# Feed-forward layers with features on partitions, and transposing DMAs in place of TensorE transposes

## The chip, the cores and the metric

The kernel runs on one core of one Trainium2 chip. The metric is the device time of one execution in microseconds (us). Before the change the median of three runs is 1394.78 us (1393.33 to 1395.5).

## The reference: what is computed

The kernel computes a forward pass and all gradients of a stack of four residual layers, alternately linear attention (A) and a gated feed-forward layer (B), with shared weights: layers 0 and 2 are A, 1 and 3 are B. There are 2048 tokens (S), 512 model features (D), 1376 hidden features (F), all tensors in bf16. Cut to what matters here:

```python
def _B_ref(x, w_gate, w_up, w_down):
    g = jnp.einsum("bsd,df->bsf", x, w_gate)
    u = jnp.einsum("bsd,df->bsf", x, w_up)
    h = _sigmoid(g) * u
    return jnp.einsum("bsf,fd->bsd", h, w_down)

x = x + _A_ref(_layernorm(x), A_wqkv, A_wo)
x = x + _B_ref(_layernorm(x), B_w_gate, B_w_up, B_w_down)
x = x + _A_ref(_layernorm(x), A_wqkv, A_wo)
x = x + _B_ref(_layernorm(x), B_w_gate, B_w_up, B_w_down)
```

Outputs are x, the gradient of x, and the gradients of the five weight matrices (summed over the two layers that share each).

## The kernel before, in words

[...] A matmul loads its stationary operand (`lhsT`, up to 128 columns) and streams its moving operand (`rhs`, up to 512 columns) past it.

The phases in the order of the program: `a_fwd(0)`, `b_fwd(1)`, `a_fwd(2)`, `b_fwd(3)`, then backward `b_bwd_p1(3)`, `a_bwd_p1(2)`, `b_bwd_p2(3)`, `b_bwd_p1(1)`, `a_bwd_p2(2)`, `a_bwd_p1(0)`, `b_bwd_p2(1)`, `a_bwd_p2(0)`. The p1 phases carry the gradient of the activations back, the p2 phases form weight gradients from tensors that earlier phases stored in DRAM.

**Feed-forward, forward (`b_fwd`, 16 tiles per layer).** For each token tile the normalised input stands transposed in `hT` (features on partitions, 128 tokens wide). `hT` is the stationary operand, and the weights `wg` and `wu` move in slices of 512, 512 and 352 columns (L621, L624): tokens come out on partitions. ScalarE makes the sigmoid and its complement (L626, L628), VectorE the product hh (L629), GpSimd a factor for the backward pass (L630). The down projection (L599) contracts over F, and so needs F on partitions: 11 TensorE transposes per tile (L587) with copies by ScalarE (L590, L592) turn `hh_t` into `hhT`. The rows go to DRAM as `ssd` and `hdd`, tokens by features.

**Feed-forward, backward (`b_bwd_p1`, 16 tiles per layer).** The same scheme: `gT` is stationary, `wdT` moves (L760), VectorE makes two products `dd` (L762, L763), 22 transposes per tile (L728) with ScalarE copies (L730, L732) make `ddT`, and 22 matmuls of 512 columns (L742) contract over F. `dd` goes to DRAM next to hh, tokens by features.

**Weight gradients (`b_bwd_p2`).** They contract over tokens, and so need tokens on partitions, as they stand in DRAM. Six groups of feature chunks (five of 256 features, one of 96), each with three sets `p_set` (hh, du, dg): 2048 rows of up to 512 bytes, 1 MB in a full set, loaded by plain DMAs on the SP queue (L811) into a pool of three buffers. A full set feeds 32 matmuls of 512 columns (L863) or 64 of 256 (L833).

**Transposed weights.** The backward pass needs all five weight matrices transposed. During the two `a_fwd` phases, `wT_groups` transposes them on TensorE (L372, L396, 196 transposes in 49 groups of four), copies them out of PSUM on VectorE and ScalarE (`evac`) and stores them to DRAM; `load_b_weights` and `load_a_weights` load them by plain DMAs at the start of the p1 phases. One buffer each is shared by `wuT` and `wqkvT`, and by `wgT` and `woT`.

**What sets the order.** The program is written phase by phase, but a planner at build time makes the final order on each engine from dependences, priorities (earlier in the program first) and assumed costs. Work of a p2 phase can therefore stand between the instructions of a p1 phase, and does (L863 among L742). On the chip each engine, and each DMA queue, goes through its list in order: an instruction that waits holds up all that follows it in that list, so a load on SP stands behind the stores before it.

Of the kernel before, what the change touches and what calls it, by code (L numbers as in the profile page):

```python
# [16 lines left out]
S = 2048  # L17
# [33 lines left out]
def kernel(  # L51
# [70 lines left out]
    for l in range(4):  # L122
        d = {}
        d["h"] = dram.tile([S, D], BF16, name=f"sv_h{l}")
        d["gbf"] = dram.tile([S, D], BF16, name=f"sv_gbf{l}")
        if l % 2 == 0:
            for nm in ("pq", "pk", "v", "o"):
                d[nm] = dram.tile([S, D], BF16, name=f"sv_{nm}{l}")
            d["dqkv"] = dram.tile([S, 3 * D], BF16, name=f"sv_dqkv{l}")
        else:  # L130
            d["ssd"] = dram.tile([S, 2, F], BF16, name=f"sv_ssd{l}")
            d["hdd"] = dram.tile([S, 3, F], BF16, name=f"sv_hdd{l}")
        k.sv[l] = d
    k.wT = dict(
        wqkvT=dram.tile([3 * D, D], BF16, name="wqkvT_d"),
        woT=dram.tile([D, D], BF16, name="woT_d"),
        wgT=dram.tile([F, D], BF16, name="wgT_d"),
        wuT=dram.tile([F, D], BF16, name="wuT_d"),
        wdT=dram.tile([D, F], BF16, name="wdT_d"),
    )  # L140
# [11 lines left out]
    with tc.tile_pool(name="wfwd", bufs=1) as wfwd:  # L152
# [17 lines left out]
        with ExitStack() as lctx:  # L170
            k.lnres = dict(
                stg=lctx.enter_context(tc.tile_pool(name="ln_stg", bufs=2)),
                hT=lctx.enter_context(tc.tile_pool(name="ln_hT", bufs=4)),
# [4 lines left out]
            if phases != "fwd":  # L178
                wtg = wT_groups(k)
                half = 26  # L180
                with tc.tile_pool(name="wt_stage", bufs=2) as wt_stage:
                    a_fwd(k, 0, lns[0], nxt=lns[1],
                          extra=lambda ps_pool: [g(wt_stage, ps_pool) for g in wtg[:half]])
                b_fwd(k, 1, lns[1], nxt=lns[2])
                with tc.tile_pool(name="wt_stage2", bufs=2) as wt_stage:
                    a_fwd(k, 2, lns[2], nxt=lns[3],
                          extra=lambda ps_pool: [g(wt_stage, ps_pool) for g in wtg[half:]])
            else:
                a_fwd(k, 0, lns[0], nxt=lns[1])
                b_fwd(k, 1, lns[1], nxt=lns[2])  # L190
                a_fwd(k, 2, lns[2], nxt=lns[3])
# [17 lines left out]
    with ExitStack() as bctx:  # L209
# [3 lines left out]
        def load_b_weights():  # L213
            k.wdT = wb.tile([P, NDC, F], BF16, name="wdT", tag="w_c")
            nc.sync.dma_start(out=k.wdT[:], in_=k.wT["wdT"].rearrange("(c p) f -> p c f", p=P))
            k.wuT = wb.tile([P, NFC, D], BF16, name="wuT", tag="w_a")
            k.wgT = wb.tile([P, NFC, D], BF16, name="wgT", tag="w_b")
            for t_sb, t_d in ((k.wuT, k.wT["wuT"]), (k.wgT, k.wT["wgT"])):
                nc.sync.dma_start(out=t_sb[:, 0:NFC - 1, :],
                                  in_=t_d[0:(NFC - 1) * P, :].rearrange("(c p) j -> p c j", p=P))  # L220
                nc.sync.dma_start(out=t_sb[0:FLAST, NFC - 1, :], in_=t_d[(NFC - 1) * P:F, :])

        def load_a_weights():
            k.woT = wb.tile([P, NDC, D], BF16, name="woT", tag="w_b")
            nc.sync.dma_start(out=k.woT[:], in_=k.wT["woT"].rearrange("(c p) j -> p c j", p=P))
            k.wqkvT = wb.tile([P, 3 * NDC, D], BF16, name="wqkvT", tag="w_a")
            nc.sync.dma_start(out=k.wqkvT[:], in_=k.wT["wqkvT"].rearrange("(c p) j -> p c j", p=P))
# [4 lines left out]
                  sets=bctx.enter_context(tc.tile_pool(name="p2sets", bufs=3)),  # L232
# [113 lines left out]
def wT_groups(k):  # L346
    nc = k.nc
    groups = []
    cnt = [0]

    def evac(dst, src):
        if cnt[0] % 2 == 0:
            nc.vector.tensor_copy(dst, src)
        else:
            nc.scalar.copy(dst, src)
        cnt[0] += 1

    for w_sb, wT_d, C in ((k.wg, k.wT["wgT"], F), (k.wu, k.wT["wuT"], F),
                          (k.wqkv, k.wT["wqkvT"], 3 * D), (k.wo, k.wT["woT"], D)):
        ncc = (C + P - 1) // P  # L360
        for cc0 in range(0, ncc, 4):
            ccs = list(range(cc0, min(cc0 + 4, ncc)))
            holder = {}
            for j, cc in enumerate(ccs):
                def g(stage, ps_pool, w_sb=w_sb, wT_d=wT_d, C=C, cc0=cc0, ccs=ccs, j=j, cc=cc, holder=holder):
                    if j == 0:
                        holder["t"] = stage.tile([P, 4, D], BF16, name="wt_st")
                    st_t = holder["t"]
                    r = min(P, C - cc * P)
                    ps = ps_pool.tile([P, NDC, P], BF16, name="wt_ps")  # L370
                    for rc in range(NDC):
                        nc.tensor.transpose(ps[0:r, rc, :], w_sb[:, rc, cc * P:cc * P + r], k.ident[:])  # L372
                    evac(st_t[0:r, j, :], ps[0:r, :, :].rearrange("p a b -> p (a b)"))
                    if j == len(ccs) - 1:
                        nfull = len([c_ for c_ in ccs if min(P, C - c_ * P) == P])
                        if nfull > 0:
                            nc.sync.dma_start(
                                out=wT_d[cc0 * P:(cc0 + nfull) * P, :].rearrange("(n p) d -> p n d", p=P),
                                in_=st_t[:, 0:nfull, :])
                        if nfull < len(ccs):  # L380
                            c_ = ccs[nfull]
                            r_ = C - c_ * P
                            nc.sync.dma_start(out=wT_d[c_ * P:c_ * P + r_, :], in_=st_t[0:r_, nfull, :])
                groups.append(g)
    for cc in range(NDC):
        holder = {}
        for fs in range(3):
            def g(stage, ps_pool, cc=cc, fs=fs, holder=holder):
                if fs == 0:
                    holder["t"] = stage.tile([P, F], BF16, name="wdt_st")  # L390
                st_t = holder["t"]
                fcs = fchunks_of_slice(fs)
                ps = ps_pool.tile([P, NDC, P], BF16, name="wt_ps")
                for i, fc in enumerate(fcs):
                    r = fc_rows(fc)
                    nc.tensor.transpose(ps[:, i, 0:r], k.wd[0:r, fc, cc * P:(cc + 1) * P], k.ident[0:r, 0:r])  # L396
                c0, w = FSL[fs]
                evac(st_t[:, c0:c0 + w], ps[:].rearrange("p a b -> p (a b)")[:, 0:w])
                if fs == 2:
                    nc.sync.dma_start(out=k.wT["wdT"][cc * P:(cc + 1) * P, :], in_=st_t[:])  # L400
            groups.append(g)
    return groups


NPRE = 2


class FwdLN:
# [7 lines left out]
    def stage(self, st):  # L416
# [10 lines left out]
        hT = R["hT"].tile([P, NDC, P], BF16, name="hT")  # L427
        transpose_blocks(k, R["ps"], hT[:], [h_t[:, c * P:(c + 1) * P] for c in range(NDC)], "vector", tag="ln_tp")
        self.hTs[st] = hT
# [5 lines left out]
    def pop(self, st):  # L435
        self.ensure(st)
        return self.hTs.pop(st)


def a_fwd(k, l, ln, nxt=None, extra=None):  # L440
    nc, tc = k.nc, k.tc
    sv = k.sv[l]
    with ExitStack() as ctx:
# [8 lines left out]
        if extra is not None:  # L452
            ps_extra = ctx.enter_context(tc.tile_pool(name=f"af_ps_extra{l}", bufs=1, space=PSUM))
# [656 lines left out]
```

## Time and profile before

| what | us |
|---|---|
| median of three runs | 1394.78 |
| the profiled execution: span from first to last instruction | 1393.1 |
| TensorE matmul busy | 1297.9 (93%) |
| VectorE busy | 679.9 (49%) |
| ScalarE busy | 647.3 (46%) |
| GpSimd busy | 250.5 (18%) |
| mean granted TensorE clock | 0.988 |
| mean DMA rate | 194 GB/s, 269.77 MB moved |

No time outside the span is on record for the profiled execution; its span stands 1.7 us below the median of the runs.

How to read the views: a row of the timeline has the start and the length in us, the engine (PE is TensorE, PEld its weight loads, DVE VectorE, ACT ScalarE, POOL GpSimd, SPq the queue of SyncE), the line of the kernel, the operation, output and inputs, the shape (partitions by columns) and the number of instructions merged into the row; a bracket tells how long the engine had been idle before and who released it. The length of a PE row includes the pipeline's tail of its last matmul; how long a group holds TensorE is read from its start to the start of the next row. A DMA row has the size of one transfer and the median time from issue to landing.

### The profile page before, as it was taken

Reading aid. Unit: us, or ns where it says so; the run is one execution under the profiler, and the core shown is the slowest. Engines: PE = TensorE matmul, PEld = TensorE weight load, DVE = VectorE, ACT = ScalarE, POOL = GpSimd, SP = SyncE. Lnnn points to the kernel's source line nnn. Section 1 sums busy time; section 2 is a strip of 40 time slices with the busy share of each in tenths; the row PEclk is TensorE's granted clock in tenths of the full one; section 3 lists DMA queues with packets and bytes.
Section 4 is the critical chain, followed back from the end, with each engine's and each line's share of the span. In section 5 each row is a group of like instructions: output and inputs, shape, how many; then the busy total and the mean of one; then the engine's idle time right before and its main releaser. Section 6 shows DMA issues by size and latency. Waiting matters only on the chain. (4 is left out here: it accounts for less than half of the span.)

```text
span 1393.1 us, 25045 instructions
## 1 busy us (share of the span) xinstructions
PE 1297.9 (93%) x9956; PEld 790.1 (57%) x9956; DVE 679.9 (49%) x1468; ACT 647.3 (46%) x1168; POOL 250.5 (18%) x413
## 2 busy tenths in 40 slices
PE   4989899998899898998999999999999999988988
PEld 2555455556455444554665677555548675556767
DVE  6664644567533355665857400456640676611111
ACT  5857576775776544443547411444431447600000
POOL 4026654105633300002100100010010101100000
PEclk9999999999999999999999999999999999999999
DMA  7622334452543497547774586964568956499745
GB/s 273 230 103 103 149 152 158 147 177 98 201 178 143 169 326 259 175 168 237 218 230 148 181 227 149 334 217 167 172 199 248 275 169 192 143 311 261 175 122 162
DMA packets 268853, 269.77 MB, mean 194 GB/s; under 512 B 24576, under 2 KB 245184, under 8 KB 268736
## 3 DMA queue, kind: packets, MB, share of 16 engines
q1 hardware_dynamic: 246272, 253.50, 57.2%
q10 hardware_dynamic: 22464, 14.68, 3.6%
q8 instruction: 78, 1.28, 0.4%
q14 instruction: 39, 0.32, 0.1%
HBM read 144.57 MB, written 123.57 MB: 192 GB/s over the span
## 5 line engine op out<-in xcount | busy, mean ns | idle before, releaser
L730 ACT COPY ddT<-T_ps 128x1024 bf16<-128x1024 bf16 (+1 forms) x96 | 83.1, 867 | 103.4 <-PE T_ps L728 103.3
L630 POOL TENSOR_TENSOR ssd_t<-hh_t,oms 128x512 bf16<-128x512 bf16 (+1 forms) x96 | 100.6, 1052 | 83.0 <-ACT oms L628 48.4
L648 DVE SCALAR_TENSOR_TENSOR junk<-t_sb,h_ld 128x512 bf16<-128x512 f32 x64 | 46.1, 720 | 137.6 <-ACT t_sb L646 136.6
L762 DVE TENSOR_TENSOR dd_t<-dhh_ps,ssd_ld 128x512 bf16<-128x512 f32 (+1 forms) x96 | 60.4, 629 | 102.0 <-PE dhh_ps L760 102.0
L742 PEld LDWEIGHTS <-ddT 128*128 128x128 bf16 (+1 forms) x704 | 66.3, 98 | 71.4 <-issue 12.5
L468 PE MATMUL mm_ps<-wqkv,hT 128*128 128x512 bf16 x384 | 100.2, 386 | 0.5 <-DVE x_108 L601 0.4
L742 PE MATMUL dh_ps<-wuT,ddT 128*128 128x512 bf16 (+1 forms) x352 | 96.5, 382 | 3.9 <-ACT t_sb L646 0.9
L833 PE MATMUL p_ps<-p_set,p_a_15354 128*128 128x256 bf16 (+1 forms) x768 | 82.5, 267 | 10.8 <-DVE dw_stg L798 10.8
L629 DVE TENSOR_TENSOR hh_t<-u_ps,ssd_t 128x512 bf16<-128x512 f32 (+1 forms) x96 | 60.7, 634 | 65.3 <-PE u_ps L624 50.3
L760 PE MATMUL dhh_ps<-wdT,gT 128*128 128x512 bf16 (+1 forms) x384 | 87.8, 364 | 5.0 <-DMA wdT<-wdT_d 4.3
L624 PE MATMUL u_ps<-wu,hT 128*128 128x512 bf16 (+1 forms) x384 | 92.4, 361 | 0.0
L621 PE MATMUL g_ps<-wg,hT 128*128 128x512 bf16 (+1 forms) x384 | 92.0, 361 | 0.4 <-DVE ostage L530 0.4
L833 PE MATMUL p_ps<-p_set,p_a_10151 128*128 128x256 bf16 (+1 forms) x768 | 81.5, 261 | 0.9 <-DMA p_set<-sv_hdd_130 0.9
L599 PE MATMUL y_ps<-wd,hhT 128*128 128x512 bf16 (+1 forms) x352 | 81.4, 380 | 0.0
L742 PE MATMUL dh_ps<-wgT,ddT 128*128 128x512 bf16 (+1 forms) x352 | 81.3, 379 | 0.0
L833 PEld LDWEIGHTS <-p_a_15354 128*128 128x128 bf16 x768 | 68.9, 100 | 21.7 <-issue 8.4
L590 ACT COPY hhT<-hhT_ps 128x512 bf16<-128x512 bf16 (+1 forms) x96 | 49.5, 515 | 58.3 <-PE hhT_ps L587 58.1
L728 PEld LDWEIGHTS <-dd_t 128*128 128x128 bf16 (+1 forms) x704 | 50.7, 101 | 40.8 <-DVE dd_t L762 18.5
L833 PEld LDWEIGHTS <-p_a_10151 128*128 128x128 bf16 x768 | 67.2, 98 | 9.2
L728 PE MATMUL T_ps<-ident,dd_t 128*128 128x128 bf16 (+1 forms) x704 | 66.4, 221 | 3.6 <-DVE dd_t L762 3.5
L838 DVE TENSOR_TENSOR dw_stg<-p_ps,dw_stg 128x512 bf16<-128x512 f32 (+1 forms) x36 | 23.4, 653 | 87.5 <-PE p_ps L833 74.4
L1038 PE MATMUL dh_ps<-wqkvT,dkvT 128*128 128x512 bf16 x256 | 65.6, 380 | 0.0
(493 smaller groups left out, 2498.3 us busy)
## 6 DMA issues: line engine op xcount, KB each, us to landing
p_set<-sv_hdd_130 SPq DMA_DIRECT2D x15, 1024.0 KB, 7.1
p_set<-sv_hdd_119 SPq DMA_DIRECT2D x15, 1024.0 KB, 6.3
sv_ssd_118<-ssd_t SPq DMA_DIRECT2D x16, 688.0 KB, 3.1
sv_ssd_129<-ssd_t SPq DMA_DIRECT2D x16, 688.0 KB, 3.1
ssd_ld<-sv_ssd_129 SPq DMA_DIRECT2D x16, 688.0 KB, 5.5
sv_hdd_130<-dd_t SPq DMA_DIRECT2D x16, 688.0 KB, 3.9
ssd_ld<-sv_ssd_118 SPq DMA_DIRECT2D x16, 688.0 KB, 6.0
sv_hdd_119<-dd_t SPq DMA_DIRECT2D x16, 688.0 KB, 3.7
```

What stands on the lines that cost most here:

```text
L468: nc.tensor.matmul(ps[:], lhsT=hT[:, kc, :], rhs=k.wqkv[:, kc, n * D:(n + 1) * D], start=(kc == 0), stop=(kc == NDC - 1))
L599: nc.tensor.matmul(y_ps[:], lhsT=T["hhT"][0:r, fc, :], rhs=k.wd[0:r, fc, :], start=(fc == 0), stop=(fc == NFC - 1))
L621: nc.tensor.matmul(g_ps[:, 0:w], lhsT=hT[:, kc, :], rhs=k.wg[:, kc, c0:c0 + w], start=(kc == 0), stop=(kc == NDC - 1))
L624: nc.tensor.matmul(u_ps[:, 0:w], lhsT=hT[:, kc, :], rhs=k.wu[:, kc, c0:c0 + w], start=(kc == 0), stop=(kc == NDC - 1))
L629: nc.vector.tensor_tensor(hh_t[:, c0:c0 + w], u_ps[:, 0:w], ssd_t[:, 0, c0:c0 + w], ALU.mult)
L630: nc.gpsimd.tensor_tensor(ssd_t[:, 1, c0:c0 + w], hh_t[:, c0:c0 + w], oms[:, 0:w], ALU.mult)
L728: nc.tensor.transpose(tps[0:r, a, i, :], dd[:, a, fc * P:fc * P + r], k.ident[:])
L730: nc.scalar.copy(ddT[:, :, fcs[0]:fcs[0] + nfull, :], tps[:, :, 0:nfull, :])
L742: nc.tensor.matmul(dh_ps[:], lhsT=T["ddT"][0:r, a, fc, :], rhs=wT[0:r, fc, :], start=(i == 0), stop=(i == n_mm - 1))
L760: nc.tensor.matmul(dhh_ps[:, 0:w], lhsT=gT[:, jc, :], rhs=k.wdT[:, jc, c0:c0 + w], start=(jc == 0), stop=(jc == NDC - 1))
L833: nc.tensor.matmul(psv[:, icl, :], lhsT=lhs_all[:, st, ic * P:(ic + 1) * P], rhs=set_t[:, st, 0:W], start=(st == 0), stop=(st == NST - 1))
L1038: nc.tensor.matmul(dh_ps[:], lhsT=lhsT, rhs=k.wqkvT[:, n * NDC + c, :], start=(i == 0), stop=(i == 3 * NDC - 1))
```

## The change

Four things are changed at once.

1. `b_fwd` works on blocks of 512 tokens (`SB`), `b_bwd_p1` on blocks of 256 (`SBB`). The weight chunks are now stationary and the tokens move, so features come out on partitions, and the transposes of hh, du and dg are gone. hh, sg, qg, du and dg are stored in DRAM as features by tokens.
2. `b_bwd_p2` loads its sets from there with `dma_start_transpose` on the SP queue, in a pool of two buffers instead of three.
3. `wT_groups` is gone; the transposed weights are loaded by `dma_start_transpose` straight from the inputs. Since F is no multiple of 128, two small DRAM tensors `wtail` are filled at the very start by four DMAs.
4. Smaller: `NPRE` 4 instead of 2 (tiles whose layer norm is made ahead), three blocks of `hT` instead of four tiles, other counts of PSUM buffers.

```diff
+    k.wtail = {nm: dram.tile([D, P], BF16, name=f"wtail_{nm}") for nm in ("wg", "wu")}
+    for nm, w_in in (("wg", B_w_gate), ("wu", B_w_up)):
+        nc.sync.dma_start(out=k.wtail[nm][:, 0:FLAST], in_=w_in[:, F - FLAST:F])
+        nc.sync.dma_start(out=k.wtail[nm][:, FLAST:P], in_=w_in[:, 0:P - FLAST])
...
-            nc.sync.dma_start(out=k.wdT[:], in_=k.wT["wdT"].rearrange("(c p) f -> p c f", p=P))
+            nc.sync.dma_start_transpose(out=k.wdT[:], in_=B_w_down[:, :])
...
+            for t_sb, w_in, nm in ((k.wuT, B_w_up, "wu"), (k.wgT, B_w_gate, "wg")):
+                nc.sync.dma_start_transpose(out=t_sb[:, 0:NFC - 1, :], in_=w_in[:, 0:(NFC - 1) * P])
+                nc.sync.dma_start_transpose(out=t_sb[:, NFC - 1, :], in_=k.wtail[nm][:, :])
...
-                  sets=bctx.enter_context(tc.tile_pool(name="p2sets", bufs=3)),
+                  sets=bctx.enter_context(tc.tile_pool(name="p2sets", bufs=2)),
...
# b_fwd
+        for sb in range(NSB):
+            hT = ln.pop_block(sb)
...
+            for fc in range(NFC):
...
-                    nc.tensor.matmul(u_ps[:, 0:w], lhsT=hT[:, kc, :], rhs=k.wu[:, kc, c0:c0 + w],
+                    nc.tensor.matmul(u_ps[0:r, :], lhsT=k.wu[:, kc, fs], rhs=hT[:, kc, :],
                                      start=(kc == 0), stop=(kc == NDC - 1))
...
-                if fs >= 1:
-                    transposes(T, fs - 1)
+                if fc in (2, 4, 6, 8):
+                    j = (fc - 2) // 2
+                    if prev is not None:
+                        finish(prev, j)
+                    if sb + 1 < NSB:
+                        ln.ensure((sb + 1) * NB + j)
+            for nm in ("sg", "qg", "hh"):
+                frows_dma(k, sv[nm], sb * SB, T[nm], True)
...
# b_bwd_p1
+            for fp in range(0, NFC, 2):
+                fcs = [fc for fc in (fp, fp + 1) if fc < NFC]
+                r = fc_rows(fcs[-1])
+                n = len(fcs)
+                dhh_ps = ps_dhh.tile([P, 2, SBB], F32, name="dhh_ps")
+                for i, fc in enumerate(fcs):
+                    for jc in range(NDC):
+                        nc.tensor.matmul(dhh_ps[0:r, i, :], lhsT=k.wdT[:, jc, fc * P:fc * P + r], rhs=gT[:, jc, :],
+                                         start=(jc == 0), stop=(jc == NDC - 1))
+                nc.vector.tensor_tensor(T["du"][0:r, fp:fp + n, :], dhh_ps[0:r, 0:n, :], sg[0:r, fp:fp + n, :],
+                                        ALU.mult)
...
+                if fp in (2, 6):
+                    j = (fp - 2) // 4
+                    if prev is not None:
+                        finish(prev, j)
+                    if (sb + 1) * SBB < S:
+                        g_stage((sb + 1) * NBB + j)
...
-def p2_set(k, R, src2d, c0, w):
+def p2_set(k, R, src2d, c0, w, transposed=False):
     t = R.sets.tile([P, NST, R.set_w], BF16, name="p2_set")
+    if transposed:
+        k.nc.sync.dma_start_transpose(out=t[:, :, 0:w], in_=src2d[c0:c0 + w, :])
+        return t
```

## The prediction, as it was put on record

> **What bounds the kernel.** I read the page's busy times first, then the timeline of TensorE inside one tile of each stage that the change rewrites, then the transfers that take over the transposing.
>
> ```profile
> PE 1297.9 (93%) x9956; PEld 790.1 (57%) x9956; DVE 679.9 (49%) x1468; ACT 647.3 (46%) x1168; POOL 250.5 (18%) x413
> PE   4989899998899898998999999999999999988988
> ```
>
> TensorE is busy for 93% of the span, in nearly every slice; the other engines stay near half. So what counts is how long the removed instructions hold TensorE, from a row's start to the next row's start. One forward tile:
>
> ```profile
> 214.94 0.40 PE L587 MATMUL hhT_ps<-ident,hh_t 128*128 128x128 bf16 x4
> 215.18 0.76 PE L621 MATMUL g_ps<-wg,hT 128*128 128x352 bf16 x4
> ...
> 216.37 0.39 PE L587 MATMUL hhT_ps<-ident,hh_t 128*128 128x128 bf16 x4
> 216.59 2.54 PE L599 MATMUL y_ps<-wd,hhT 128*128 128x512 bf16 x11
> 218.97 0.33 PE L587 MATMUL hhT_ps<-ident,hh_t 128*128 128x128 bf16 x3
> 219.14 0.39 PE L318 MATMUL ln_tp<-ident,hstage 128*128 128x128 bf16 x4
> ```
>
> The reader is to see that there is no idle bracket: each transpose pushes back what follows. The groups hold TensorE for 0.24, 0.22 and 0.17 us, 0.63 per tile. One backward tile (its groups stand at 572.05, 576.31, 576.98, 577.80 and 578.24 us; two of them):
>
> ```profile
> 572.05 0.50 PE L728 MATMUL T_ps<-ident,dd_t 128*128 128x128 bf16 x6
> 572.39 0.39 PE L318 MATMUL gT_ps<-ident,gstage 128*128 128x128 bf16 x4
> ...
> 577.80 0.39 PE L728 MATMUL T_ps<-ident,dd_t 128*128 128x128 bf16 x4
> 578.02 0.38 PE L742 MATMUL dh_ps<-wuT,ddT 128*128 128x512 bf16 x1
> ```
>
> They hold it for 0.34, 0.24, 0.22, 0.22 and 0.22: 1.24 us per tile. Last, a weight-gradient phase, and the loads that feed it between 812 and 868 us:
>
> ```profile
> 826.01 7.07 PE L863 MATMUL p_ps<-p_a_10156,p_set 128*128 128x512 bf16 x32
> 832.92 14.14 PE L833 MATMUL p_ps<-p_set,p_a_10151 128*128 128x256 bf16 x128
> 846.89 7.07 PE L863 MATMUL p_ps<-p_a_10156,p_set 128*128 128x512 bf16 x32
> ```
> ```profile
> p_set<-sv_hdd_130 SPq DMA_DIRECT2D x6, 1024.0 KB, 6.0
> p_set<-sv_hdd_130 SPq DMA_DIRECT2D x3, 384.0 KB, 4.0
> ```
>
> A set of 1 MB is used up in 6.9 to 7.0 us, without a pause between sets, and its load lands 6.0 us after issue (4.0, 5.9 and 7.1 at least, median and most, over all nine). With three buffers a load has two sets' time, 13.9 us, to arrive.
>
> **Transposes taken off TensorE.** 32 forward tiles x 0.63 = 20.2 us; 32 backward tiles x 1.24 = 39.7; the weights' 49 groups of four, at 0.22 each (a row at 40.21, the next at 40.43), 10.8. Sum 70.7 us. TensorE's recorded waits in front of them (L587 6.8, L728 3.6) total 10.4; something else will be late at some of these places, so I count half, 5. The ScalarE copies behind them, the `evac` copies and the stores of the transposed weights go too; they lie beside TensorE's work and count for nothing, nor is any cover lost with them.
>
> **Columns added.** From the rows above 512 columns cost 0.216 us (6.91 us / 32) and 256 cost 0.109 (13.97 / 128), so more weight loads per column cost almost nothing. Forward, a block of four tiles streams 88 x 512 = 45056 columns instead of 8 x 1376 x 4 = 44032, because the last chunk of 96 features costs a whole pass: 1024 more in each of 8 blocks, 3.5 us. Backward 44 x 256 = 11264 instead of 11008 in each of 16 blocks, 1.7 us, and 704 matmuls at 1 ns over the half price, 0.7. Together +6.
>
> **Start.** Four DMAs are put on SP ahead of the first load of x, on which the first LayerNorm waits. SP's rows there take 0.39 to 0.48 us each, so at least 1.8 us if nothing else is behind. They move 2048 short rows; the row nearest to that is the 384 KB set, 2048 rows of 192 bytes, at 4.0 us. If the planner puts them later, nothing. Bounds 0 and 5, I take 3.
>
> **Transposed sets, the unknown.** No row shows a transposing DMA. Its result has 128 tokens on partitions, so I assume that each row of 2048 tokens is read in 16 pieces of 256 bytes: 4096 pieces where the plain load has 2048 of 512. The two rows above differ only in bytes: 2.0 us for 640 KB, and 2.8 us for 2048 pieces and everything fixed. The shortest landing in the issue view is 2.2 us; with that as the fixed part, 2048 pieces are worth 0.6 us and a transposed set lands in 6.6. From below: 6.0, as a plain one; no gain, because the bytes are the same. From above: the rate of the 192-byte set, 4.0 x 1024 / 384 = 10.7 us. I take 6.6, nearest to the row of the same size.
>
> With two buffers a load is issued when its buffer is used up, 0.2 us after the set's end (812.04 to 812.23), and is needed one set later: it may take 6.7. The median then just fits, but plain landings reach 1.2 us over their median; I take 0.6 us of stall per set, 30 full sets in both layers, +18 (bounds 0 and (10.7 - 6.7) x 30 = 120). The six small sets are used up in 2.7 to 3.5 us and land in about 4.6: 1.3 x 6 = 8; half is hidden, where the next phase's matmuls can be put between: +4.
>
> [...]
>
> **Transposed weights.** At the start of the backward pass TensorE waits for `wdT`, whose plain load lands in 6.7 us:
>
> ```profile
> 489.47 3.14 PE L760 MATMUL dhh_ps<-wdT,gT 128*128 128x512 bf16 x7 [4.33 <-DMA wdT<-wdT_d]
> ```
>
> Scaled by 6.6 / 6.0, that is 0.7 us more. `wuT` and `wgT` follow on the same queue; at 1 MB in 6.6 - 2.2 = 4.4 us the three (4 MB) are in about 19.5 us after 482.8, at 502. The first block's 44 matmuls and two pairs of the next take about 7 us from 490, so `wgT` is wanted at about 499: 4 us. In layer 1 the loads were issued at 633, long ahead. Two attention phases start with `woT`: 1 us each. Together +7, bounds 0 and 20 (10.7 in place of 6.6).
>
> **What I cost at nothing.** Stores and loads of features by tokens move the same bytes in shorter rows; the DMA engines are 66% busy in that stage (487 to 640 us), and the cover is TensorE's block of 14.7 us. In a backward block VectorE has six pairs of products (0.60 us per full instruction) and two LayerNorm chains (2.3 us each), 12.1 us with the casts, against 14.7 on TensorE; three buffers of `dhh_ps` are the cover. The layer norms of a forward block, four now before its first matmul, are hidden by the block before, whose matmuls last 28 us.
>
> **Sum.** Against the profiled span: 1393.1 - 70.7 - 5 + 6 + 3 + 18 + 4 + 7 = 1355.4. The median of the runs lies 1.7 above that span: 1357 us.
>
> **Rivals.**
> (1) All transfers are hidden: only the transposes, their waits and the columns count, 1393.1 - 70.7 - 10.4 + 6 = 1318, 1320 on the scale of the runs. For it: TensorE has other phases' work to put between (L863 stands among L742 at 572.61). A tile of the backward stage also lasts 9.23 us (569.67 to 578.90) where its rows hold TensorE for about 8.75, and if that gap goes in 16 tiles more is gained, 8 us: down to about 1310.
> (2) VectorE becomes the bound of the backward stage: it goes in order, and its chain waits on ScalarE and GpSimd (3.05 us in front of L648 at 582.34). If 1 us per block is lost, 16 blocks give 16 us: 1373. Against it: 49% busy.
> (3) The other side, slower: transposed loads take longer than a set's compute. The place is `b_bwd_p2`, where the third buffer is gone. Without the +18 the sum is 1339, so the gain is used up at 55 us, 1.8 us per set, a landing over 8.5 us. At 10.7 it is 1393.1 - 70.7 + 6 + 5 + 20 + 120 + 8, 1481, 1483 on the scale of the runs. For it: plain loads keep the engines 69% busy in this phase already, the pieces are shorter, and SP works in order, so a transpose that occupied SP would also hold back the stores and the partial gradients behind it (TensorE already waits 5.49 us at 1260 for such a chain). Against it: only an unseen cost makes it.
> (4) The change does not take what it says off TensorE, if the planner had put the transposes in idle time: 1393. The rows without brackets speak against it.
>
> **Chances.** The forecast with its surroundings (1340 to 1366) 0.38; (1) 0.20; (2) and smaller stalls up to 1391, 0.09; (4), within 0.2% (about what a measurement of this kernel tells from no change), 0.03; (3) 0.30, of which a third lies beyond its price. The range goes from 1310 to 1483 and leaves out some 15 in 100. Faster 0.67, same 0.03, slower 0.30.
>
> **What would show it.** L587, L728, L372 and L396 are gone, and TensorE's busy time is some 65 us or more lower. L811 shows a landing: below 6.7 us rival (1), 6.7 to 8.5 the forecast, above rival (3), with idle time of L833 and L863 put down to `p_set`. Idle time of L760 put down to VectorE would be rival (2). I am wrong in kind if TensorE's stalls grow inside the forward stage, or if plain transfers land later because transposes are in flight.

## The result: slower by half a per cent, where 2.7% less time was forecast

The changed kernel takes 1400.95 us (median of ten runs, 1397.8 to 1406.23), the kernel before 1394.74 us on the same chip (1391.82 to 1397.98): a ratio of 1.0045, 95% interval 1.0028 to 1.0062. The forecast was 1357, its range 1310 to 1483; the chance given to slower was 0.30.

The profiled execution spans 1396.9 us, 3.8 more than before. First the page's busy times and two rows of its timeline:

```profile
PE 1234.9 (88%) x8960; PEld 750.9 (54%) x8960; DVE 666.1 (48%) x1435; ACT 497.4 (36%) x871; POOL 250.2 (18%) x405
...
PE   3978999997999389998989889999989999749888
...
PEclk9989999999999789999999999999999999979999
```

TensorE's busy time fell by 63.0 us, near the forecast ("some 65 us or more"; 64.7 without the waits), though at a lower mean granted clock, 0.967 where it was 0.988 before. But its idle time inside the span grew from 95 to 162 us. Two holes are new, the 3 in the fourteenth slice (about 454 to 489 us) and the 7 and 4 around 1220 us, and in both the granted clock falls too, to 0.71 in the first and to 0.73 between 1225 and 1260 us. The view of TensorE's waits names what ended the idle time (us in total, times, longest):

```profile
PE gT_ps L303 <- DMA gstage<-in_grad_out_dram: 27.5, 1, 27.5
PE p_ps L781 <- DMA p_set<-sv_dg: 24.5, 8, 11.4
...
PE p_ps L811 <- DMA p_set<-sv_hh: 10.3, 2, 9.3
```

Before, TensorE waited 0.9 us for sets in all, and for no load of a gradient tile:

```profile
PE p_ps L833 <- DMA p_set<-sv_hdd_130: 0.9, 1, 0.9
```

After, with 5.3 us for `du`, the sets make TensorE wait 40 us; the first gradient tile of the backward pass makes it wait 27.5. Where the time is gained and lost is seen from the ends of TensorE's work in each stage. The last column is an experiment told below, in which no DMA transposes anything:

| stage | before, us | after | difference | nothing transposed by DMA |
|---|---|---|---|---|
| start to the end of the last forward block | 482.8 | 465.8 | -17.0 | 460.5 |
| from there to the first `dhh` matmul | 6.7 | 30.1 | +23.4 | 14.9 |
| `b_bwd_p1(3)`, to its last `dh` | 153.1 | 127.2 | -25.9 | 126.5 |
| `a_bwd_p1(2)` | 145.1 | 154.6 | +9.5 | 144.3 |
| `b_bwd_p2(3)` | 89.1 | 104.7 | +15.6 | 89.4 |
| `b_bwd_p1(1)` | 151.4 | 122.2 | -29.2 | 123.5 |
| `a_bwd_p2(2)`, `a_bwd_p1(0)` | 188.6 | 195.0 | +6.4 | 192.3 |
| `b_bwd_p2(1)` and the last phase | 172.4 | 192.7 | +20.3 | 174.2 |

(Weight-gradient work that stood between a p1 phase's matmuls moved to the next stage: 5.0 us of the first -25.9, L863, and 6.5 of the -29.2, L885.) The rewritten backward stages gained at least what they should, by the count of the prediction 18.7 us each. The time is lost at the start of the backward pass, in `a_bwd_p1(2)`, and in the two `b_bwd_p2` stages, where sets are loaded.

**How a transposing DMA looks.** Rows of the tile `p_set`, durations on SP (minimum, median, maximum in ns), after and then before:

```profile
L757 SPq DMA_TRANSPOSE p_set<-sv_hh x12: 1399/4388/9666, 559.6 to 1309.9; - x12
L757 SPq DMA_TRANSPOSE p_set<-sv_du x12: 1285/4307/9212, 641.6 to 1318.0; - x12
L757 SPq DMA_TRANSPOSE p_set<-sv_dg x12: 1403/4752/12067, 650.3 to 1321.4; - x12
```
```profile
L811 SPq DMA_DIRECT2D p_set<-sv_hdd_130 x18: 359/360/879, 534.9 to 868.0; - x18
```

This is the row that the prediction lacked. A plain load occupies SP for 0.36 us and moves on its own; a transposing one occupies SP for 4.3 to 4.8 us in the median and for up to 12, some two thirds of the time until its data has landed. From issue to landing the two kinds are close in the median, before and after:

```profile
p_set<-sv_hdd_130 SPq DMA_DIRECT2D x15, 1024.0 KB, 7.1
p_set<-sv_hdd_119 SPq DMA_DIRECT2D x15, 1024.0 KB, 6.3
...
p_set<-sv_hh SPq DMA_TRANSPOSE x12, 6.4
p_set<-sv_du SPq DMA_TRANSPOSE x12, 7.0
p_set<-sv_dg SPq DMA_TRANSPOSE x12, 7.4
```

The forecast's 6.6 us is within that, and the median over all 36 is 6.9. But the median was the wrong thing to ask, for two reasons. The sets for which TensorE waited more than 2 us landed late: 7.3 to 10.0 us after issue in three cases, 18.6 and 19.1 in two (from the issue on SP to the end of TensorE's wait); only a last small set took 5.4. And whatever stands behind a transpose in SP's list waits for it, the first gradient tile for 22.5 us from the issue of `wdT` on.

**The start of the backward pass**, on SP and then on TensorE:

```profile
467.69 8.33 SPq L201 DMA_TRANSPOSE wdT<-in_B_w_down_dram  x1
476.07 5.66 SPq L205 DMA_TRANSPOSE wuT<-in_B_w_up_dram  x1
...
483.08 5.67 SPq L205 DMA_TRANSPOSE wgT<-in_B_w_gate_dram  x1
488.80 1.26 SPq L206 DMA_TRANSPOSE wgT<-wtail_wg  x1
490.16 0.53 SPq L600 DMA_DIRECT2D gstage<-in_grad_out_dram  x1
```
```profile
493.29 0.58 PE L303 MATMUL gT_ps<-ident,gstage 128*128 128x128 bf16 x4 [27.48 <-DMA gstage<-in_grad_out_dram]
```

The first gradient tile is issued 22.5 us after `wdT`, behind all weights. Before, the same load was issued in the middle of the forward pass:

```profile
350.37 0.37 SPq L666 DMA_DIRECT2D gstage<-in_grad_out_dram  x1
```

Now nothing of the backward pass is loaded until the last forward block is done.

**The first weight-gradient phase**, SP and then TensorE:

```profile
792.24 7.41 SPq L757 DMA_TRANSPOSE p_set<-sv_hh  x1
...
801.57 5.91 SPq L757 DMA_TRANSPOSE p_set<-sv_du  x1
...
810.01 6.31 SPq L757 DMA_TRANSPOSE p_set<-sv_dg  x1
...
819.32 5.31 SPq L757 DMA_TRANSPOSE p_set<-sv_hh  x1
```
```profile
791.98 8.83 PE L781 MATMUL p_ps<-p_set,p_a 128*128 128x256 bf16 x64 [4.26 <-DMA p_set<-sv_dg]
...
819.98 8.83 PE L781 MATMUL p_ps<-p_set,p_a 128*128 128x256 bf16 x64 [3.20 <-DMA p_set<-sv_dg]
```

From 792.24 to 819.32 SP has no pause over 0.2 us: three transposes hold it for 19.6 us, and the loads of the next phase and the partial gradients take the other 7.4. So a group of three sets costs 27.1 us of SP, and TensorE needs 21 for it. The loads are issued 0.8 to 4.7 us after their buffer is free, and land after 8.0 to 10.0. Whether SP is the bound here is not shown by this: the DMA engines are full as well (the time of their packets is 1.11 of what 16 engines have in this stretch), and with plain sets, in experiment 3 below, TensorE is busy for only 21.3 us of a like stretch (780 to 807 us there) too.

**The last feed-forward phase**, where the loads for the last phase come on ACT's queue at the same time:

```profile
1213.10 12.07 SPq L757 DMA_TRANSPOSE p_set<-sv_dg  x1
1232.25 9.67 SPq L757 DMA_TRANSPOSE p_set<-sv_hh  x1
1244.73 9.21 SPq L757 DMA_TRANSPOSE p_set<-sv_du  x1
```
```profile
1232.23 9.34 PE L781 MATMUL p_ps<-p_set,p_a 128*128 128x256 bf16 x64 [11.40 <-DMA p_set<-sv_dg]
1250.88 8.51 PE L811 MATMUL p_ps<-p_a,p_set 128*128 128x512 bf16 x32 [9.31 <-DMA p_set<-sv_hh]
```

The DMA engines are full here (share 1.15 between 1225 and 1260), and the transposes last twice as long. TensorE is busy for 18.5 of these 35 us. The chain of waits runs through two landings: the `dg` set lands 19.1 us after its issue, the `hh` set is issued then and lands 18.6 us later. Of all 30 full sets, the 17 during whose issue the share was 1.02 or less hold SP for 4.0 to 5.5 us, the 13 at 1.07 or more for 5.3 to 12.1. So it is full DMA engines that go with long transposes.

### The profile page after: what moved, and what is told of

It is laid out like the page before. It is cut to its first block, busy times and chain, and to the rows that moved or that the text cites. A ratio compares the mean times of both kernels' runs of the same rounds, so it can differ in the third digit from the quotient of the medians.

```text
span 1396.9 us, 22644 instructions
## 1 busy us (share of the span) xinstructions
PE 1234.9 (88%) x8960; PEld 750.9 (54%) x8960; DVE 666.1 (48%) x1435; ACT 497.4 (36%) x871; POOL 250.2 (18%) x405
## 3 DMA queue, kind: packets, MB, share of 16 engines
q8 instruction: 70, 1.15, 0.3%
## 5 line engine op out<-in xcount | busy, mean ns | idle before, releaser
L781 PE MATMUL p_ps<-p_set,p_a 128*128 128x256 bf16 (+1 forms) x1920 | 210.8, 268 | 34.5 <-DMA p_set<-sv_dg 24.5
L781 PEld LDWEIGHTS <-p_a 128*128 128x128 bf16 x1920 | 173.8, 99 | 64.1 <-DMA p_set<-sv_dg 26.3
L562 POOL TENSOR_TENSOR qg_t<-hh_t,oms 128x512 bf16<-128x512 bf16 (+1 forms) x88 | 101.1, 1152 | 80.1 <-DVE hh_t L561 74.0
L811 PE MATMUL p_ps<-p_a,p_set 128*128 128x512 bf16 (+1 forms) x352 | 84.8, 388 | 10.3 <-DMA p_set<-sv_hh 10.3
L700 PE MATMUL dhh_ps<-gT,wdT 128*128 128x256 bf16 (+1 forms) x704 | 86.9, 276 | 7.5 <-DVE dg_t L704 6.2
L556 PE MATMUL u_ps<-hT,wu 128*128 128x512 bf16 (+1 forms) x352 | 90.3, 379 | 1.8 <-DVE hh_t L561 1.8
L553 PE MATMUL g_ps<-hT,wg 128*128 128x512 bf16 (+1 forms) x352 | 90.3, 379 | 1.6 <-DVE kvbdT L494 1.6
L670 PE MATMUL dh_ps<-wuT,du_t 128*128 128x512 bf16 (+1 forms) x352 | 85.3, 383 | 0.3 <-DVE du_t L702 0.3
L670 PE MATMUL dh_ps<-wgT,dg_t 128*128 128x512 bf16 (+1 forms) x352 | 82.1, 380 | 0.0
L533 PE MATMUL y_ps<-wd,hh_t 128*128 128x512 bf16 (+1 forms) x352 | 81.6, 379 | 0.0
L700 PEld LDWEIGHTS <-wdT 128*128 128x128 bf16 (+1 forms) x704 | 68.3, 101 | 23.3 <-DVE dg_t L704 12.7
```

The source lines that it names most:

```text
L533: nc.tensor.matmul(y_ps[:], lhsT=T["hh"][0:r, fc, j * P:(j + 1) * P], rhs=k.wd[0:r, fc, :], start=(fc == 0), stop=(fc == NFC - 1))
L553: nc.tensor.matmul(g_ps[0:r, :], lhsT=k.wg[:, kc, fs], rhs=hT[:, kc, :], start=(kc == 0), stop=(kc == NDC - 1))
L556: nc.tensor.matmul(u_ps[0:r, :], lhsT=k.wu[:, kc, fs], rhs=hT[:, kc, :], start=(kc == 0), stop=(kc == NDC - 1))
L562: nc.gpsimd.tensor_tensor(T["qg"][0:r, fc, :], T["hh"][0:r, fc, :], oms[0:r, :], ALU.mult)
L670: nc.tensor.matmul(dh_ps[:], lhsT=T[nm][0:r, fc, j * P:(j + 1) * P], rhs=wT[0:r, fc, :], start=(i == 0), stop=(i == n_mm - 1))
L700: nc.tensor.matmul(dhh_ps[0:r, i, :], lhsT=k.wdT[:, jc, fc * P:fc * P + r], rhs=gT[:, jc, :], start=(jc == 0), stop=(jc == NDC - 1))
```

## The experiments

The theory from these rows (A): transposing loads hold SP, and so delay the sets and whatever is queued with them. Rivals: the third buffer alone is missing (B), and the start of the backward pass is late because no SBUF is free for loads ahead of it (C). Each kernel is compared with the kernel before on the same chip, ratios with 95% intervals; differences to the changed kernel are between medians, also where the chip was another one (the kernel before took 1393.5 to 1394.7 us beside all of them).

**1. The order of loads in the first backward phase.** In `b_bwd_p1(3)`:

```diff
-    k.load_b_weights()
+    if l != 3:
+        k.load_b_weights()
...
         lds = {0: load(0)}
+        if l == 3:
+            k.load_b_weights()
```

> Theory A (a transposing DMA holds the SP queue for as long as it moves data, so what stands behind it is late): with the first gradient load and the first sg and qg loads ahead of the transposes of wuT and wgT, TensorE's wait for gstage at the start of the backward pass falls from 27.5 us to about 14 us (the 8.3 us of wdT still stand in front) and the kernel gains 12 to 15 us. Theory B (the engines are saturated there, the order on the queue does not matter): the wait stays above 22 us and the gain is under 5 us.

1392.09 us, ratio 0.9981 (0.9967 to 0.9996): 8.9 us less than the changed kernel. The wait for `gstage` is 14.3 us long instead of 27.5. The planner kept `wdT` ahead of the gradient tile and put only the other weights behind it, so half of the wait went. The gain is under the expected 12 to 15, since the stage behind, `b_bwd_p1(3)`, takes 5 us more (132.3, before this edit 127.2). The place in the queue matters, and it isn't all.

**2. A third set buffer.**

```diff
-sets=bctx.enter_context(tc.tile_pool(name="p2sets", bufs=2)),
+sets=bctx.enter_context(tc.tile_pool(name="p2sets", bufs=3)),
```

> Only the pool of the sets has three buffers again. Theory A (a transposed set lands in about 6.8 us, as long as a set's compute, and only the third buffer's absence makes that late): TensorE's waits for p_set fall from 40 us to under 12 and the kernel gains 22 to 30 us. Theory B (the transposes move too few bytes per us for the phase): the queue only gets longer, waits for p_set stay above 30 us and the gain is under 8 us.

1379.32 us, ratio 0.9895 (0.9871 to 0.9919): 21.6 us less, just under the 22 of theory A. TensorE's waits for `p_set` fall from 40 us to about 1. What is left in the set phases is put down to `dw_stg`, with the stored partial gradients behind it (12.7 us).

**3. and 4. Sets by plain DMAs, with two buffers and with three.** The transposition is left out, so the sets hold the same bytes untransposed.

```diff
-k.nc.sync.dma_start_transpose(out=t[:, :, 0:w], in_=src2d[c0:c0 + w, :])
+flat = src2d.rearrange("f s -> (f s)").rearrange("(a b) -> a b", b=F)
+k.nc.sync.dma_start(out=t[:, :, 0:w], in_=flat[:, c0:c0 + w].rearrange("(n p) f -> p n f", p=P))
```

> The sets are loaded by plain DMAs of the same size from the same tensors read as rows of 1376, with two buffers: the transposition of hh, du and dg is left out, so the feed-forward weight gradients are those of scrambled sets. If the transposition is what costs (landing and held queue): TensorE's waits for p_set fall from 40 us to under 15 and the kernel gains 20 us or more. If two buffers are what costs, whatever the kind of load: a plain load still needs 6 us of the 6.7 that there are, the waits stay at 15 to 30 us and the gain is 5 to 15 us.

> Plain loads of the sets (the transposition of hh, du and dg is left out, the feed-forward weight gradients are those of scrambled sets) and three buffers. With two buffers the plain loads gave 1368.7 us, three buffers with transposes 1379.3. If the held queue and the longer landing are one cost that a third buffer partly covers, the fourth corner lies near 1360 to 1366: the third buffer is worth 3 to 9 us to plain loads and 21.6 to transposing ones. If the third buffer and the kind of load are worth the same independently, it would lie near 1347.

Two buffers: 1368.67, ratio 0.9814 (0.9792 to 0.9836). Three: 1358.66, ratio 0.9734 (0.971 to 0.9758), a little below what was expected. With experiment 2 this makes a square, medians in us:

| sets | two buffers | three buffers | the third is worth |
|---|---|---|---|
| transposing DMAs | 1400.95 | 1379.32 | 21.6 |
| plain DMAs | 1368.67 | 1358.66 | 10.0 |
| transposing costs | 32.3 | 20.7 | |

Both matter, and either covers part of the other. A missing buffer alone (B) explains 10 us; transposing costs 20.7 even where TensorE hardly waits for a set, and there landing can't be the difference. With two buffers it can be a part of it: the feed-forward sets land in 6.1 us plain and in 6.9 transposed (medians), and the prediction's 6.7 us of room lies between. Even the plain sets with two buffers make TensorE wait 18.7 us, more than the 15 expected; 10.2 of it are two sets of the last phase, which land after 13.1 and 15.4 us.

**5. Weights transposed on TensorE again.** `wT_groups`, its stores and the plain loads of the five weights come back, with the PSUM buffers of `a_fwd` that go with them (one pool 5 instead of 6, another 1 instead of 2); everything else is as after the change.

```diff
-nc.sync.dma_start_transpose(out=k.wdT[:], in_=B_w_down[:, :])
+nc.sync.dma_start(out=k.wdT[:], in_=k.wT["wdT"].rearrange("(c p) f -> p c f", p=P))
...
+a_fwd(k, 0, lns[0], nxt=lns[1],
+      extra=lambda ps_pool: [g(wt_stage, ps_pool) for g in wtg[:half]])
```

> The transposed weights are made by TensorE and loaded by plain DMAs again, all else as in the changed kernel. Theory A (the five transposes on SP hold up the first loads of the backward pass): the wait of 27.5 us falls to about 6, TensorE gets 10.8 us of transposes back, part of which fill idle time of the attention phases: 10 to 18 us faster than the changed kernel. Theory B (the wait has another cause, the last stores of the forward pass): the wait stays over 20 us and the kernel is 5 to 10 us slower.

1381.69 us, ratio 0.9906 (0.988 to 0.9933): 19.3 us less, a little more than theory A expected. But the wait at the start of the backward pass hardly went (21.9 us, now put down to `sg_ld`), against theory A. SP in that stretch:

```profile
472.73 1.35 SPq L215 DMA_DIRECT2D wdT<-wdT_d  x1
...
475.57 4.65 SPq L221 DMA_DIRECT2D wuT<-wuT_d  x1
...
480.73 4.03 SPq L221 DMA_DIRECT2D wgT<-wgT_d  x1
484.86 0.38 SPq L678 DMA_DIRECT2D gstage<-in_grad_out_dram  x1
```

The two 96-row loads (L221) hold SP for 4 to 5 us, with 2.6 MB issued in the 3 us before the first of them, and the gradient tile is issued 12 us after `wdT`. In the profiles the gain is spread: 3.4 us at the start, 5.7 before the first `dhh`, 8.6 in `a_bwd_p1(2)`, 6.7 in the last stage; in the forward pass the stretches up to the last projection of the two attention layers take 15 us more, those behind them 6.6 less. So for this wait theory C has to be asked directly.

**6. A place of its own for the first gradient tile.** Experiment 1, and the first two gradient tiles are loaded into 2 KB per partition of their own ahead of `b_fwd(3)`.

```diff
+k.gpre = resid.tile([P, 2, D], BF16, name="gpre")
...
+nc.sync.dma_start(out=k.gpre[:], in_=dram_batch(g_in, 0, 2))
 b_fwd(k, 3, lns[3])
```

> As the reordered kernel (gradient, sg and qg loads ahead of the transposes of wuT and wgT), and the first gradient tile has 2 KB per partition of its own, so that its load can be issued during the forward pass. Theory C (at the end of the forward pass no SBUF is free, so every load of the backward pass is issued after the last down projection, and then stands in one queue): the wait for gstage disappears, dhh starts when wdT lands, about 478 to 480 us instead of 483 with the order alone, and the kernel gains another 3 to 5 us. Theory A alone (only the queue's order counts): no further gain, under 1.5 us.

1386.37 us, ratio 0.9934 (0.9911 to 0.9957): 14.6 us less than the changed kernel, 5.7 of it from the early load. TensorE:

```profile
464.65 0.39 PE L305 MATMUL gT_ps<-ident,gpre 128*128 128x128 bf16 x4
...
477.18 3.17 PE L707 MATMUL dhh_ps<-gT,wdT 128*128 128x256 bf16 x14 [5.88 <-DMA wdT<-in_B_w_down_dram]
```

The gradient is transposed right behind the last forward matmul, and the next late thing is `wdT`, issued only after the last forward block, as it is in the kernel before too. So C holds for the wait for `gstage`: a place of its own ends it. The edit also moves the load ahead in the program, but before the change the load stood in the same place of the program as after it, and ran ahead all the same (350.4 us). That SBUF is what was short is concluded from these two facts; no view shows it. As a price of this wait the 5.7 us are not exact: in the profiles the first `dhh` comes 4.4 us sooner after the forward pass than in experiment 1, and `b_bwd_p1(3)` takes 3.4 us longer.

**7. Partial gradients on the other queue.** Three set buffers, and the loads of the stored partial gradients are issued by ACT, so that no transpose stands ahead of them.

```diff
-R.eng().dma_start(out=pv, in_=dwp_ap)
+nc.scalar.dma_start(out=pv, in_=dwp_ap)
```

> Three buffers, and in the two final weight-gradient phases the loads of the first layer's partial gradients go to the queue of ScalarE instead of SP. If transposes on SP hold those loads back (they stand behind transposes of 8 to 12 us in the kernel with three buffers), VectorE's waits for them and with them TensorE's 12.7 us of waits for dw_stg fall under 4 us, and the kernel gains 7 to 12 us over 1379.3. If the DMA engines are simply saturated there, the waits stay over 9 us and the gain is under 3 us.

1393.35 us, ratio 0.9988 (0.9973 to 1.0003): 14.0 more than experiment 2, against the expectation. TensorE's waits for `dw_stg` grew (17.6 and 9.4 us), and the transposes between 1206 and 1262 us took 8 to 13 us. On ACT the small loads stand among the megabytes of the last phase, and TensorE's waits for `dw_stg` of 9.43, 8.55 and 9.07 us end at 1229, 1246 and 1260 us.

**8. Order and third buffer together.**

> The order of the first backward loads and three buffers together. The two gains were 8.9 and 21.6 us by themselves and lie in different phases, so they should add: 1369 to 1373 us.

1370.48 us, ratio 0.9829 (0.9797 to 0.9862). The two gains add up (8.9 and 21.6 of 30.5).

**9. The weights' part alone, on the kernel before.** The diff's first two parts, and nothing else of the change.

> The kernel before with one part of the change alone: the transposed weights come by transposing DMAs straight from the inputs (with the four small DMAs at the start), and the 196 TensorE transposes of the weights are gone; the feed-forward layers and the sets stay as before. Theory A, the weights' part is a loss by itself: restoring it gave 19.3 us back on the changed kernel, so here it costs 10 us or more, 1405 to 1414. Theory B, it is a loss only beside the rest of the change (no SBUF left for loads ahead, SP held by transposed sets as well): here the start's 3.5 us and some 4 us at the start of the backward pass stand against up to 10.8 us of transposes, of which part filled idle time: 1388 to 1397. I take B.

The time is 1408.11 us, ratio 1.0103 (1.0086 to 1.012): 14.0 more than before. I had taken the other side; this part is a loss by itself. The forward pass began 3.2 us later and ended only 1.7 us earlier, although 196 transposes were gone.

**10. and 11. Weights on TensorE and three buffers, without and with the order of experiment 1.**

> The changed kernel with the weights transposed on TensorE again, as before, and three buffers for the sets. Apart these two edits gave 19.3 and 21.6 us. If they remove different waits they add up: 1360. If both only give SP the same slack in the weight-gradient phases, the second is worth less: 1367 to 1376. I take the first within 3 us.

> As the run with weights on TensorE and three buffers, and in the first backward phase the weights' loads are issued after the first gradient tiles and the first stored factors. With transposing loads this order was worth 8.9 us. If the wait at the start of the backward pass comes from the place of the loads in one queue, whatever their kind, it is worth 8 to 14 us here too, and the time is 1346 to 1355. If plain loads do not gain from the order, it stays at that of the run without it, within 3 us.

They take 1366.65 us, ratio 0.9802 (0.9781 to 0.9823), and 1356.68 us, ratio 0.9727 (0.9707 to 0.9747). The first pair overlaps (34.3 us together, 40.9 apart), against my expectation of 1360. Most of the overlap is in the last stage, where the two edits gain 6.7 and 12.9 us apart and 15.5 together. The order is worth 10.0 with plain loads too. The last kernel leaves nothing out and is 37.4 us faster than the kernel before (1394.1 there): it beats both kernels.

**12. Loads of the last phase later.** Three set buffers; the 4 MB for the last phase are issued by SP, the first after the third of six groups in the program's order.

```diff
-set_w=2 * P, dma=[nc.scalar], pfx="ta")
+set_w=2 * P, pfx="ta")
...
+        if mid is not None and g0 == 3 * nper:
+            mid()
```

> The changed kernel with three set buffers, and the loads for the last phase (4 MB of o and gradient tiles, 1 MB sets of dqkv), which ran on ACT's queue from the start of the last feed-forward weight-gradient phase, are put on SP, the first of them after the third of its six groups. Theory A, in that phase the transposes last 8 to 12 us because these loads fill the DMA engines at the same time: then the stalls there (some 15 us with three buffers) go, transposes take 4 to 5 us, 1364 to 1371. Theory B, the transposes hold SP for as long whatever else moves: 1376 to 1382, or more if the last phase's first tiles now come late (up to 10 us).

1376.45 us, ratio 0.9871 (0.9853 to 0.9889), 2.9 less than experiment 2 and inside the range of theory B. The planner spread these loads between the sets from 1205 us on, so they did not leave the stretch, and its transposes still held SP for 5.6 to 7.9 us there. The test did not separate what it was meant to.

**13. and 14. Weights not transposed at all**, in the kernel before and in the changed kernel: the same bytes by plain loads, without `wtail`; the transposition of the weights is left out.

> The kernel before without the TensorE transposes of the weights; the weight tiles of the backward pass are loaded by plain DMAs of the same size from the inputs (their transposition is left out), and the four small DMAs at the start are gone. It prices the 10.8 us that the prediction took off alone. Theory A, as predicted, each transpose pushes back what follows: 1394.1 - 10.8 = 1383. Theory B, part of them filled time in which TensorE would have waited in the attention layers (with transposing loads the forward pass ended 1.7 us earlier although it began 3.2 later, so 5 us): 1388 to 1391. I take B.

> The changed kernel with plain loads of the weight tiles (their transposition is left out) and without the four small DMAs at the start; no transposes of weights anywhere, the sets still by transposing DMAs. Weights on TensorE gave 1381.69. If those transposes cost 5 to 8 us there, this gives 1373 to 1377, and 24 to 28 us is what the weights' transposing loads cost in the changed kernel. If the loss came from something else in that run, such as its other order of SP, this stays near 1382 or above.

They take 1391.44 us, ratio 0.9979 (0.9966 to 0.9992), and 1375.14 us, ratio 0.9854 (0.983 to 0.9878): the first just above the expectation taken, the second inside. The weights' term of the sum is now in parts, medians in us:

| weights | rest as before | rest as after |
|---|---|---|
| transposing DMAs | 1408.11 | 1400.95 |
| transposed on TensorE | 1394.1 to 1394.7 | 1381.69 |
| not transposed | 1391.44 | 1375.14 |
| transposes on TensorE cost | 3 | 6.6 |
| transposing DMAs cost | 16.7 | 25.8 |

The 25.8 and the 6.6 are not exact: the four runs of experiment 14 lie between 1369.11 and 1381.86 us, and its profiled execution is 16.8 us shorter than that of the changed kernel. Of these 16.8, 3.0 are at the start, 6.2 before the first `dhh` and 6.8 in `a_bwd_p1(2)`, where the next weights are loaded. With no transposed weight at all, TensorE still waits 21.3 us for the first loads of the backward pass.

**15. Nothing transposed by DMA.** Plain weights, plain sets, three buffers, the order of experiment 1; both transpositions are left out.

> The changed kernel with plain loads of weights and sets (both transpositions left out), three set buffers, and the weights' loads after the first gradient tiles in the first backward phase. It asks whether the 65 us that left TensorE come through when nothing is transposed by DMA. If the parts add up: 1358.66 with plain sets and three buffers, less 8.9 for the order and less 15 to 20 for the weights: 1330 to 1335. If a new bound stands behind them (VectorE in the backward stage, or no free SBUF at its start), 1340 or more. I take the first.

1333.22 us, ratio 0.9565 (0.9551 to 0.9579), as expected. Its page has TensorE at 1224.4 us (92% of 1329.8), and the stages of the first table's last column. The rewritten feed-forward layers give what the count of removed instructions says. The start of the backward pass still takes 8.2 us more than before (14.9 against 6.7), though nothing is transposed there.

## Why the prediction was wrong

*Transposes off TensorE, columns added (-70.7 and +6).* Right as instructions: 63.0 us of busy time went (73.5 in experiment 15, at a granted clock of 0.982), and experiment 15 shows 61 us of time gained once nothing is transposed by DMA, with the order of experiment 1 as a help that the forecast did not have. The 5 us for waits in front of the transposes were not measured by themselves. The step fails for the weights' 10.8 us: they are worth 3.0 us in the kernel before and 6.6 in the changed one. The row without a bracket at 40 us showed transposes that push others back; it did not show that the attention layers would wait for VectorE and ScalarE instead, once these fillers are gone. Experiment 13 shows it: the last projections of the two attention layers end 8.3 and 10.4 us earlier than before, but TensorE's waits behind them grow from 4.2 to 8.8 us (71 to 130 us) and from 9.3 to 15.3 (300 to 365 us), and the forward pass ends only 2.6 us earlier.

*Start (+3).* Right: TensorE's first matmul comes 3.5 us later. The four DMAs hold SP for 2.7 us of that (0.81 to 3.51 us), with 0.61 to 0.66 us each.

*Transposed sets (+18 and +4).* Two steps failed. One is a single landing of 6.6 us for all sets, with 0.6 us of stall. It was scaled from a stretch with a DMA share of 0.69, where plain sets land in 6.0 us; the page of before has 7.1 for that layer's sets. After, TensorE waited for sets that landed after 7.3 to 10.0 us in the first phase and 18.6 and 19.1 in the last, and these last two alone are 20.7 of the 40 us of waits. The other is "a load is issued when its buffer is used up, 0.2 us after the set's end". That was read from a queue of 0.36 us rows. With rows of 4 to 12 us a load is issued when SP gets to it, 0.8 to 4.7 us late in the first phase, and the loads between are held as well. The two terms were 22 us together; two transposing buffers in place of three plain ones cost 42.3 (1400.95 - 1358.66), and transposing alone 32.3 with two buffers. How the 32.3 divide between the two steps is not shown.

*Transposed weights (+7).* Transposing them cost 16.7 to 25.8 us, with the start's 3 in it, where the two terms had 10. The step took only `wdT`'s landing to be on the path, since the trace of before shows TensorE wait for that alone. It missed that the weights hold SP for 22 us at the start of the backward pass, with the gradient tile behind all of them.

*A term that the sum doesn't have.* The larger part of the loss at the start of the backward pass is not from transposing: of the 23.4 us in the first table 6.2 go with plain weights (experiment 14), 17.2 stay. The prediction missed that in the kernel before the gradient tile had been loaded 130 us ahead and that it would not be now. Experiment 6 shows that a place of its own brings it ahead again. The issue time of `gstage` in the trace of before, and the change's larger buffers, could have raised the question.

*Rivals.* VectorE as the bound (2) is not seen: `dhh` waits 6.2 us for it. Rival (3) had the right side, a right place and even the mechanism ("a transpose that occupied SP would also hold back the stores and the partial gradients"). I tied it to landing over 8.5 us for all sets; the medians are 6.4 to 7.4, and it came true in the few sets that landed after 9.5 to 19.1. Of the start of the backward pass it says nothing. The mark of being wrong in kind, plain transfers landing later, appeared in part: `gstage` lands in 4.7 us, before in 3.5.

*The sum.* From experiment 15, adding back 8.9 for the order, 32.3 and 10.0 for the sets and 25.8 for the weights gives 1410, 9 us above the measured 1401: the parts overlap by about that much, within the few us by which such medians are uncertain.

*What stays open.* With three buffers transposing the sets still costs 20.7 us though TensorE waits about 1 us for them. In the profiles 10 us of it are in pauses over 1 us, the rest in shorter ones that I could not put down to one cause; 6.4 us are in each of the two `b_bwd_p2` stages, 4.2 in `b_bwd_p1(3)` and 2.8 in `a_bwd_p1(2)`. The long transposes go with full DMA engines (a share of 1.07 or more), but no run emptied the engines there, so experiments 7 and 12 did not settle how much of the loss is the held queue's and how much the engines'. The same holds for the 32.3 us with two buffers.

## What to carry to other kernels

Before moving work from an engine to a kind of DMA that the trace doesn't show, price two things, not one: how long until the data lands where the DMA engines are fullest (here up to 19.1 us, with a median of 6.9), and how long the instruction holds the queue that issues it (here 4.3 to 4.8 us in the median, where a plain load takes 0.36), and then list all that stands behind it there. Work taken off the busiest engine gains only where it stood on the path: fillers in a stage that waits for other engines cost little (here 3.0 to 6.6 us for 10.8 us of them). And a change that takes larger buffers can lose loads that ran far ahead (here the first gradient tile, issued at 350 us before and at 490 after); look up when the first loads of the next stage are issued now, and whether they still have a place.

## What the runs showed of the hardware

- A transposing load of a set held its queue for some two thirds of the time until its data had landed: 4.0 to 5.5 us for 1 MB at a DMA share up to 1.02, 5.3 to 12.1 us at 1.07 or more, where a plain one takes 0.36. From issue to landing transposed and plain sets are close (medians 6.9 and 6.1 us with two buffers), but the kernel takes 32.3 us longer with the transposed ones.
- Plain loads held SP as well: 4.65 us for 96 rows of a weight, with 2.6 MB issued in the 3 us before (experiment 5).
- Behind its long pauses TensorE was slow for a while. A row of 64 matmuls of 256 columns lasts 7.16 us after pauses of 0.76 and 1.39 us, 8.83 after 3.20, and 9.34 after 11.40; in the first 4 us of the last of these the granted clock is 0.50, behind it 0.95; in the first 4 us after the two short pauses it is 1.00. The two rows behind the longer pauses take 1.7 and 2.2 us more than those behind the short ones.
